# When eight weight pieces are converted: w_out in batches 1 to 3 instead of 0 to 2

## The chip, the core and the metric

The kernel runs on one core of a Trainium2 chip. The metric is device time in microseconds (us): the median of several executions. A profiled execution gives, beside its own time, a trace of every engine: PE (matrix multiply) with PEld (its weight load), DVE (vector), ACT (scalar), POOL (GpSimd) and SP (which here only issues DMAs).

## The reference, cut to what matters

Three stages follow each other. Attention works on 8 batches of 8 heads, 512 tokens and 32 state rows; it gives 4,608 rows of 512. A mixture of experts sends every row through one of 8 experts and scales it. A bilinear block ends it:

```python
xread  = softmax(scale * x @ state.T) @ state
sread  = softmax(scale * state @ x.T) @ x
x      = rows of concat([xread, sread])          # 4608 x 512
e      = argmax(x @ w_gate);  x = gate * (relu(x @ w1[e]) @ w2[e])
out    = (((x @ wa) * (x @ wb)) @ w3) @ w_out
```

`w3` is 1024 x 1024 and `w_out` 1024 x 512, and nothing non-linear stands between them, so the kernel multiplies them with each other first (`wo = w3 @ w_out`) and uses the product in the last block. Weights such as `w3` and `w_out` arrive as 64-bit floats and must be turned into 32-bit floats on the chip.

## The kernel before

**Stages.** Attention comes first, one pass of a loop over the batches `b` = 0 to 7. Routing of the rows follows, then the experts, then the bilinear block. PE multiplies in pairs of a high and a low part (`split` makes the pair from an f32 tile: a copy on ACT, a subtraction on DVE or POOL).

**The loop over batches.** Each pass emits seven steps in the order given by `order`, "xswrguf": `x` loads the tokens of batch b+3 (4 DMAs, buffer of 4 batches, so x of batch 4 needs batch 0's buffer back, which `read(0)` gives back); `s` is `softmaxes(b+1)` (transposes, scores, exponentials; DVE takes the maxima and sums); `w` loads and converts rows of `w3` (list `w3`: one eighth in batches 1, 2, 3, two in 4, one in each of 5, 6, 7, each as two halves of 128x512); `r` is `read(b)` (transposes of the weights of attention, products, `x_rows` written); `g` the gates of the state rows; `u` loads and converts pieces of `w_out`, those that list `wu` gives to this batch; `f` fuses an eighth of `w3` with all of `w_out` (one in batch 5, two in batch 7, five more during routing).

**A piece.** `load_w_out(i)` issues one DMA of 512 KB on SP into a `raw` buffer (`wu_raw`, 3 buffers shared with the halves of `w3`), and `convert` makes f32 of it: on ACT `Abs` into `wu_top` (L225) and a scaled copy into the f32 tile (L239), on DVE a maximum (L228), a shift (L230) and a merge (L233), on POOL an integer addition (L240). `split_w_out` then copies it on ACT (L177) and subtracts (L178) on DVE for pieces 0 and 5, on POOL for the six others. The f32 tiles (`wst`) have two buffers. Halves of `w3` go through the same `convert` as `w_raw` and `w_top`. The first reader of the finished pieces is the product `pwo` of the first `fuse`.

**What sets the order.** The program is not run in the order in which it is emitted. The tile framework plans it: every instruction has a place in emission order, shifted by `prio` (softmaxes and reads 300 places ahead, `w` 300 places back, `u` unshifted); a planner walks through the whole program in planned time and gives each engine the best-placed instruction that it thinks ready. Each engine's list is then fixed, and the chip runs each list strictly in order: an instruction that waits holds back all that stand behind it on its engine.

```python
prio = kn("prio", [0] * 7)
for b in range(B):
    for c in kn("order", "xsurgwf"):
        p_ = prio["xsurgwf".index(c)]
        with tc.high_priority(offset=p_) if p_ else ExitStack():
            steps[c](b)
```

Of the kernel before, what the change touches and what calls it, by code (L numbers as in the profile page):

```python
# [52 lines left out]
def tile_attention_moe_bilinear(  # L53
# [21 lines left out]
    B, H, S, D = x.shape  # L75
# [8 lines left out]
    NTT = NT // P  # L84
    NX = B * NC_
    SCALE = 1.0 / float(D) ** 0.5
    KN = {'e_wu': ['vector', 'gpsimd', 'gpsimd', 'gpsimd', 'gpsimd', 'vector', 'gpsimd', 'gpsimd'], 'prio': [0, 300, 0, 300, 0, -300, 0], 'w3b': 11, 'q_sr': 'sync', 'e_an': ['gpsimd', 'gpsimd'], 't_psr': 'B', 't_pl': 'B', 'q_wo': 'sync', 'wu': [0, 0, 0, 1, 1, 1, 2, 2], 'early': 7, 'ohb': 17, 'q_raw': 'sync', 'e_sT': ['vector', 'scalar'], 'e_tr': ['scalar', 'any', 'any', 'vector'], 'b_top': 2, 'w3': [1, 2, 3, 4, 4, 5, 6, 7], 't_psl': 'C', 't_pw3': 'A', 't_pst': 'C', 'b_sT': 2, 't_pS': 'A', 'b_a2': 1, 'e_add': ['gpsimd', 'gpsimd', 'gpsimd', 'gpsimd', 'gpsimd', 'gpsimd'], 'b_aT': 6, 'q_xr': 'sync', 'b_xr': 4, 'b_h': 10, 'q_std': 'sync', 'q_an': 'gpsimd', 'e_low': ['vector', 'gpsimd'], 't_pxr': 'CB', 'e_abs': 'scalar', 'ahead': 1, 'b_a': 1, 't_psT': 'A', 'b_xT': 1, 'fuse': [5, 7, 7, 7], 'e_xT': ['any', 'any', 'vector', 'any'], 'order': 'xswrguf', 'ahead0': 2}
    def kn(name, default):
        return KN.get(name, default)

# [219 lines left out]
    with ExitStack() as c1:  # L310
# [122 lines left out]
        wu = [fu.tile([P, KF, DM], F32R, name=f"wu{i}", bufs=1) for i in range(2)]  # L433
# [257 lines left out]
        prio = kn("prio", [0] * 7)  # L691
# [882 lines left out]
```

## Time and profile before

| | us |
|---|---|
| median of 3 runs (1165.36 to 1170.16) | 1168.14 |
| the profiled execution | 1171.04 |
| its span, first to last instruction | 1169.1 |
| PE busy in it | 1118.7 |
| DVE, ACT, POOL busy in it | 664.0, 450.7, 398.2 |

How to read it: the span is the part of the profiled execution that the trace covers; all starts in the trace are counted from its beginning. Attention fills about the first 145 us, routing the time to about 190 us, experts and bilinear block the rest. A busy share over the whole span mixes these stages, so the rows below are taken from stretches.

### The profile page before, as it was taken

How to read it: one execution, taken by the hardware profiler on the slowest of the kernel's cores; microseconds unless marked ns; L12 is line 12 of the kernel's file. 1: busy time of each engine (PE TensorE's matmuls, PEld its weight loads, DVE VectorE, ACT ScalarE, POOL GpSimd, SP SyncE). 2: the span in 40 equal slices, each digit the busy share in tenths (PEclk: the TensorE clock that was granted, in tenths of full speed). 3: DMA queues.
4: the chain of work that ended last, by engine and by line, in shares of the span. 5: the costliest groups of instructions: out<-in, count | busy, mean ns of one | idle time of the engine just before them, and what ended most of it. 6: DMA issues, size and time to landing. Idle time of an engine off the chain costs nothing. (4 is left out here: it accounts for less than half of the span.)

```text
span 1169.1 us, 18224 instructions
## 1 busy us (share of the span) xinstructions
PE 1118.7 (96%) x6880; PEld 982.7 (84%) x6880; DVE 664.0 (57%) x1206; ACT 450.7 (39%) x807; POOL 398.2 (34%) x383
## 2 busy tenths in 40 slices
PE   6888998999999999999999999999999999999995
PEld 4666777999999999987888888898888889889994
DVE  4999787636464546464855547343644545463341
ACT  3778644435454545454413223121412322131121
POOL 2555326114140322132001434623543453344222
PEclk9899999999999999999999999999999999999998
DMA  7786425546566666677414645443544445343431
GB/s 227 223 254 200 160 96 209 201 153 228 187 228 211 215 216 201 233 221 242 158 35 176 248 152 199 171 174 141 205 174 160 156 180 189 135 181 132 184 127 57
DMA packets 85008, 211.55 MB, mean 181 GB/s; under 512 B 12976, under 2 KB 42672, under 8 KB 79920
## 3 DMA queue, kind: packets, MB, share of 16 engines
q1 hardware_dynamic: 62256, 167.53, 42.2%
q10 hardware_dynamic: 17024, 24.42, 5.7%
q0 software_dynamic: 5632, 18.35, 4.5%
q8 instruction: 56, 0.92, 0.3%
q14 instruction: 40, 0.33, 0.1%
HBM read 166.23 MB, written 44.04 MB: 180 GB/s over the span
## 5 line engine op out<-in xcount | busy, mean ns | idle before, releaser
L183 PE MATMUL p<-w_x,w 128*128 128x448 f32 (+1 forms) x1638 | 338.6, 360 | 0.0
L183 PEld LDWEIGHTS p<-w_x,w 128*128 128x128 f32 x1638 | 303.7, 188 | 25.4
L183 PE MATMUL py<-h,w 128*128 128x288 f32 (+1 forms) x1152 | 197.9, 329 | 3.0 <-ACT y L1087 3.0
L183 PE MATMUL ph<-x,w 128*128 128x288 f32 (+2 forms) x1248 | 196.5, 316 | 2.9 <-DVE h L1025 2.7
L183 PEld LDWEIGHTS ph<-x,w 128*128 128x128 f32 x1248 | 179.4, 188 | 15.6 <-DVE h L1025 4.4
L183 PEld LDWEIGHTS py<-h,w 128*128 128x128 f32 x1152 | 173.8, 188 | 19.2 <-ACT y L1087 4.6
L178 DVE TENSOR_TENSOR w<-raw,w 128x1024 fp32r<-128x1024 f32 x80 | 96.9, 1237 | 74.6 <-ACT w L177 72.5
L1434 POOL TENSOR_TENSOR ab<-u,s 128x448 f32<-128x448 f32 (+1 forms) x40 | 47.6, 1189 | 259.3 <-DVE u L1432 170.4
L183 PE MATMUL po<-w_wo,aa 128*128 128x512 f32 x480 | 125.3, 393 | 1.9 <-ACT aa L177 1.0
L183 PEld LDWEIGHTS po<-w_wo,aa 128*128 128x128 f32 x480 | 89.7, 188 | 18.8 <-DVE aa L178 1.7
L177 ACT CAST w<-raw 128x1024 fp32r<-128x1024 f32 x80 | 81.6, 1050 | 51.6 <-DMA raw<-in_moe_w 46.8
L177 ACT CAST ab<-ab 128x384 fp32r<-128x384 f32 (+1 forms) x40 | 19.7, 493 | 184.4 <-POOL ab L1440 174.0
L240 POOL TENSOR_TENSOR wab<-wab,wab_top 128x512 int32<-128x512 int32 x16 | 20.7, 1292 | 179.5 <-DVE wab_top L233 151.5
L183 PE MATMUL po<-w_wo,ab 128*128 128x512 f32 x336 | 79.6, 391 | 0.4 <-DVE o L1466 0.4
L183 PEld LDWEIGHTS po<-w_wo,ab 128*128 128x128 f32 x336 | 62.9, 188 | 13.9 <-DVE o L1466 0.8
L997 POOL DMA_INDIRECT xg<-x_rows,gidx x38 | 45.7, 1202 | 83.3 <-PE pxg L1003 66.7
L1437 DVE TENSOR_TENSOR u<-u,p 128x448 f32<-128x448 f32 (+1 forms) x40 | 24.3, 606 | 84.4 <-PE p L183 84.3
L1438 POOL TENSOR_TENSOR ab<-u,s 128x448 f32<-128x448 f32 (+1 forms) x40 | 48.3, 1208 | 49.2 <-DVE u L1437 49.2
L1025 DVE SCALAR_TENSOR_TENSOR h<-ph,h 128x288 fp32r<-128x288 f32 (+2 forms) x104 | 51.2, 502 | 20.8 <-ACT h L1024 20.3
L1024 ACT ACTIVATE h<-ph 128x288 fp32r<-128x288 f32 (+2 forms) x104 | 44.5, 447 | 42.6 <-PE ph L183 30.8
L183 PE MATMUL pwo<-wu,w3T 128*128 128x512 f32 x192 | 50.2, 411 | 3.4 <-POOL w3T L178 2.9
L1440 POOL TENSOR_TENSOR ab<-ab 128x448 f32<-128x448 f32 (+1 forms) x40 | 48.9, 1222 | 3.1
(291 smaller groups left out, 1441.0 us busy)
## 6 DMA issues: line engine op xcount, KB each, us to landing
w<-w_rows SPq DMA_DIRECT2D x39, 1792.0 KB
raw<-in_moe_w SPq DMA_DIRECT2D x80, 512.0 KB
x<-in_x SPq DMA_DIRECT2D x32, 256.0 KB
w_raw<-in_moe_w SPq DMA_DIRECT2D x16, 512.0 KB
x_rows<-xr SPq DMA_DIRECT2D x32, 256.0 KB
w_rows<-wh_s ACTq DMA_DIRECT2D x32, 256.0 KB
y<-y_T SPq DMA_DIRECT2D x8, 896.0 KB
w_rows<-wh_w ACTq DMA_DIRECT2D x32, 192.0 KB
```

What stands on the lines that cost most here:

```text
L177: nc.scalar.copy(hi, src)
L178: (engine or nc.vector).tensor_tensor(lo, src, hi.bitcast(F32), op=ALU.subtract)
L183: m = nc.tensor.matmul(o, l[a], r[b], start=start and i == 0, stop=stop and i == 2)
L240: nc.gpsimd.tensor_tensor(wi, wi, top, op=ALU.add)
L997: gathered = nc.gpsimd.indirect_dma_start(out=x[0:r], out_offset=None, in_=x_rows, in_offset=bass.IndirectOffsetOnAxis(ap=gidx[0:r, t - s0 ...
L1024: nc.scalar.activation(hl[0], src, AF.Relu)
L1025: nc.vector.scalar_tensor_tensor(out=hl[1], in0=src, scalar=0.0, in1=hl[0].bitcast(F32), op0=ALU.max, op1=ALU.subtract)
L1434: gpsimd(b2, u3, s5, op=ALU.add)
L1437: vector(u4, u2, p3, op=ALU.add)
L1438: gpsimd(a2, u4, s5, op=ALU.add)
L1440: gpsimd(ab[:, n : 2 * n], a2, b2, op=ALU.mult)
```

## The change

One list of settings changes: the eight pieces of `w_out`, given to batches 0, 0, 0, 1, 1, 1, 2, 2 before, are given to 1, 1, 1, 2, 2, 2, 3, 3. No instruction is added or removed, no engine, queue or buffer changes.

```diff
-    'wu': [0, 0, 0, 1, 1, 1, 2, 2]
+    'wu': [1, 1, 1, 2, 2, 2, 3, 3]
```

The list is used where batches are given their pieces and where the loop emits them:

```python
for i, b_ in enumerate(kn("wu", [0, 0, 1, 1, 2, 2, 3, 3])):
    WU[b_].append(i)
...
"u": lambda b: ([(load_w_out(i), split_w_out()) for i in WU[b]]),
```

## Rows read from the trace of the kernel before

**Rows 1.** The page: busy time of each engine, share of the span, instructions.
```profile
PE 1118.7 (96%) x6880; PEld 982.7 (84%) x6880; DVE 664.0 (57%) x1206; ACT 450.7 (39%) x807; POOL 398.2 (34%) x383
```

**Rows 2.** Windows: stretch, length, busy PE, PEld, DVE, ACT, POOL, granted clock, DMA share, GB/s.
```profile
23.00:42.00 19.00, 13.40 (x146) 10.17 (x144) 13.90 (x32) 13.10 (x27) 7.46 (x6) 0.73 0.57 190
42.00:117.00 75.00, 63.74 (x745) 46.11 (x745) 74.97 (x203) 60.42 (x130) 40.91 (x36) 1.00 0.75 231
```

**Rows 3.** Timeline of ACT: start, length, line, operation, idle before it and releaser.
```profile
26.21 0.66 ACT L225 ACTIVATE wu_top<-wu_raw 128x512 f32<-128x512 f32 x1 [5.83 <-DMA wu_raw<-in_moe_w_out]
...
28.58 1.06 ACT L140 COPY a2T<-pa2T 128x512 f32<-128x512 f32 x2
```

**Rows 4.** Timeline of DVE around pieces 0 to 2, and of later scores.
```profile
21.55 0.41 DVE L556 TENSOR_SCALAR_CACHE_REDUCE sT<-psT 128x256 f32<-128x256 f32 x1
...
26.90 0.43 DVE L228 TENSOR_SCALAR wu_top<-wu_top 128x512 f32<-128x512 f32 x1 [3.90 <-ACT wu_top L225]
...
36.69 0.67 DVE L178 TENSOR_TENSOR wu<-wu,wu 128x512 fp32r<-128x512 f32 x1
...
42.78 0.41 DVE L556 TENSOR_SCALAR_CACHE_REDUCE sT<-psT 128x256 f32<-128x256 f32 x1
...
105.05 0.41 DVE L556 TENSOR_SCALAR_CACHE_REDUCE sT<-psT 128x256 f32<-128x256 f32 x1
```

**Rows 5.** Timeline of PE: the stall, the first fuse, the last read.
```profile
23.75 0.49 PE L576 MATMUL pS<-ident,sT 128*128 128x128 f32 x3
29.20 1.94 PE L632 MATMUL psr<-x,a2T 128*32 128x64 f32 x64 [4.96 <-ACT a2T L140]
...
121.73 5.15 PE L183 MATMUL pwo<-wu,w3T 128*128 128x512 f32 x21
...
138.20 1.10 PE L632 MATMUL psr<-x,a2T 128*32 128x64 f32 x64
```

**Rows 6.** Timeline of SP's queue: DMA issues.
```profile
19.14 1.41 SPq L208 DMA_DIRECT2D wu_raw<-in_moe_w_out  x3
31.20 1.92 SPq L328 DMA_DIRECT2D x<-in_x  x4
...
123.17 0.33 SPq L208 DMA_DIRECT2D w_raw<-in_moe_w  x1
```

**Rows 7.** Tile wu_top: durations in ns, least, median, most, first and last start.
```profile
L228 DVE TENSOR_SCALAR wu_top<-wu_top x8: 411/427/1530, 26.9 to 80.8; 128x512 f32<-128x512 f32 x8
L230 DVE TENSOR_SCALAR wu_top<-wu_top x8: 364/416/817, 29.2 to 82.6; 128x512 int32<-128x512 int32 x8
L233 DVE SCALAR_TENSOR_TENSOR wu_top<-wu_raw,wu_top x8: 677/684/1531, 31.0 to 84.8; 128x512 int32<-128x512 int32 x8
```

**Rows 8.** Windows of DVE on wu_top alone: busy, clock, DMA; last their sum.
```profile
23.00:42.00 19.00, 5.29 (x9) 0.73 0.57 190
...
sum 79.00, DVE 15.98; mean DVE 3.20
```

**Rows 9.** Windows on w_top alone: busy DVE, ACT, POOL, clock, DMA.
```profile
42.00:117.00 75.00, 21.46 (x33) 7.59 (x11) 14.60 (x11) 1.00 0.75 231
```

**Rows 10.** Timeline of POOL: the last subtraction of a piece.
```profile
90.53 1.44 POOL L178 TENSOR_TENSOR wu<-wu,wu 128x512 fp32r<-128x512 f32 x1
```

**Rows 11.** Windows of all engines around the stall, columns as in rows 2.
```profile
24.00:29.00 5.00, 0.24 (x3) 0.01 (x1) 1.36 (x4) 2.76 (x5) 0.00 (x0) 0.82 0.39 158
29.00:37.00 8.00, 7.15 (x83) 5.90 (x84) 8.00 (x17) 5.35 (x12) 5.48 (x4) 0.50 0.60 160
37.00:42.00 5.00, 5.00 (x52) 3.26 (x50) 4.54 (x12) 4.99 (x12) 1.98 (x2) 0.95 0.60 233
```

**Rows 12.** Waits of ACT from 42 to 130: total us, times, longest.
```profile
ACT w L239 <- DMA w_raw<-in_moe_w: 5.7, 6, 1.8
...
ACT wu L239 <- DMA wu_raw<-in_moe_w_out: 2.2, 2, 1.2
```

**Rows 13.** Waits of PE from 200 to the end, columns as in rows 12.
```profile
PE py L183 <- ACT y L1087: 3.0, 6, 0.9
PE ph L183 <- DVE h L1025: 2.7, 4, 0.9
```

More of the change, by code (lines that the diff above doesn't have):

```diff
@@ L86, in tile_attention_moe_bilinear @@
     SCALE = 1.0 / float(D) ** 0.5
-    KN = {'e_wu': ['vector', 'gpsimd', 'gpsimd', 'gpsimd', 'gpsimd', 'vector', 'gpsimd', 'gpsimd'], 'prio': [0, 300, 0, 300, 0, -300, 0], 'w3b': 11, 'q_sr': 'sync', 'e_an': ['gpsimd', 'gpsimd'], 't_psr': 'B', 't_pl': 'B', 'q_wo': 'sync', 'wu': [0, 0, 0, 1, 1, 1, 2, 2], 'early': 7, 'ohb': 17, 'q_raw': 'sync', 'e_sT': ['vector', 'scalar'], 'e_tr': ['scalar', 'any', 'any', 'vector'], 'b_top': 2, 'w3': [1, 2, 3, 4, 4, 5, 6, 7], 't_psl': 'C', 't_pw3': 'A', 't_pst': 'C', 'b_sT': 2, 't_pS': 'A', 'b_a2': 1, 'e_add': ['gpsimd', 'gpsimd', 'gpsimd', 'gpsimd', 'gpsimd', 'gpsimd'], 'b_aT': 6, 'q_xr': 'sync', 'b_xr': 4, 'b_h': 10, 'q_std': 'sync', 'q_an': 'gpsimd', 'e_low': ['vector', 'gpsimd'], 't_pxr': 'CB', 'e_abs': 'scalar', 'ahead': 1, 'b_a': 1, 't_psT': 'A', 'b_xT': 1, 'fuse': [5, 7, 7, 7], 'e_xT': ['any', 'any', 'vector', 'any'], 'order': 'xswrguf', 'ahead0': 2}
+    KN = {'e_wu': ['vector', 'gpsimd', 'gpsimd', 'gpsimd', 'gpsimd', 'vector', 'gpsimd', 'gpsimd'], 'prio': [0, 300, 0, 300, 0, -300, 0], 'w3b': 11, 'q_sr': 'sync', 'e_an': ['gpsimd', 'gpsimd'], 't_psr': 'B', 't_pl': 'B', 'q_wo': 'sync', 'wu': [1, 1, 1, 2, 2, 2, 3, 3], 'early': 7, 'ohb': 17, 'q_raw': 'sync', 'e_sT': ['vector', 'scalar'], 'e_tr': ['scalar', 'any', 'any', 'vector'], 'b_top': 2, 'w3': [1, 2, 3, 4, 4, 5, 6, 7], 't_psl': 'C', 't_pw3': 'A', 't_pst': 'C', 'b_sT': 2, 't_pS': 'A', 'b_a2': 1, 'e_add': ['gpsimd', 'gpsimd', 'gpsimd', 'gpsimd', 'gpsimd', 'gpsimd'], 'b_aT': 6, 'q_xr': 'sync', 'b_xr': 4, 'b_h': 10, 'q_std': 'sync', 'q_an': 'gpsimd', 'e_low': ['vector', 'gpsimd'], 't_pxr': 'CB', 'e_abs': 'scalar', 'ahead': 1, 'b_a': 1, 't_psT': 'A', 'b_xT': 1, 'fuse': [5, 7, 7, 7], 'e_xT': ['any', 'any', 'vector', 'any'], 'order': 'xswrguf', 'ahead0': 2}
     def kn(name, default):
```

## The prediction

> **What bounds the kernel.** I read the page first, then the windows of the first 200 us, then the engines' timelines where a window showed idle time, and last the waits. Over the span PE is busy 96% [rows 1], which suggests that work on DVE cannot matter. The windows correct that. From 42 to 117 us, in attention, DVE is busy 74.97 of 75 us while PE has 11.3 us free [rows 2]: in this stretch DVE sets the pace, and every microsecond of DVE work there is a microsecond of time, as long as the engine never waits. The conversions of w_out and w3 run in this same stretch.
>
> Just ahead of it, from 23 to 42 us, DVE is idle for 19 - 13.90 = 5.10 us [rows 2]. The timelines show why. ACT reaches the first operation of piece 0 (L225) and stands 5.83 us until its DMA has landed; the copies a2T that read(0) needs stand behind it in ACT's list and run at 28.58 [rows 3]. PE had finished the transposes at about 24.2 and waits 4.96 us for a2T; DVE waits 3.90 us for the same piece [rows 4, 5]. So in the kernel before, the very pieces that the change moves cause the one real stall of attention. That is the argument for a gain, and the question is whether moving the pieces to batch 1 takes them away from there.
>
> **What the change does, part by part.** Nothing is added or removed: per piece one DMA issue on SP, three operations each on ACT (L225, L239, L177) and DVE (L228, L230, L233, plus L178 for pieces 0 and 5), one or two on POOL. Only the place in the planning order falls, by one batch.
>
> *Whether pieces 0 to 2 start later.* In emission order their three DMAs are moved behind the loads of x for batch 4, the writes of read(0) and of softmaxes(2) on SP, and their operations behind those of softmaxes(2) and read(1) on every engine. But emission order is not issue order. The last half of w3 belongs to batch 7 and is put back by another 300 places, yet its DMA is issued at 123.17, 15 us before the read of batch 7 at 138.20 [rows 5, 6]. Work whose buffer is free is issued far ahead of its batch when nothing better placed is ready. At 19.14 that is the position of pieces 0 to 2: all three raw buffers are empty, and the next load of x is not issued before 31.20, since it needs the buffer that read(0) gives back at 29.20 or later [rows 5, 6]. I see nothing better placed for SP to issue then, nor for ACT, which sat idle, and the halves of w3 are placed further back still. So I take it that the three DMAs keep their place at about 19, ACT keeps L225 ahead of a2T, and the stall stays: a change of 0 us. The other end of this unknown is that they really go behind the loads of x; that is the first rival.
>
> *Pieces 3 to 7.* They already wait for raw buffers and for the two f32 tiles, not for their place. After them come in both kernels the same halves of w3. Where a piece is now beaten by an operation of softmaxes or of a read, it runs some operations later; DVE executes the same sum. Cost 0, as long as they are finished in time: the last subtraction ends at 90.53 + 1.44 = 91.97 and the first fuse starts at 121.73 [rows 5, 10], so 29.8 us cover the delay. From score to score a batch takes (105.05 - 42.78) / 4 = 15.6 us [rows 4]; a whole batch of delay uses half of the cover. Without this cover the fuse would wait for whatever is missing, but it needs two batches for that.
>
> *Who runs beside whom.* The same 128x512 operation takes 0.41 us at best and 1.53 at worst (L228), and L230 and L233 spread in the same manner [rows 7]. Over the eight pieces DVE spends 15.98 us on wu_top [rows 8], and at the medians it would be 8 x (0.427 + 0.416 + 0.684) = 12.2: 3.8 us are lost to something beside them. A new order can remove these 3.8 or double them. I take 0, since neither engine's amount of work changes, and keep plus and minus 3.8 us as the bounds. The Trainium skill, page "SBUF — State Buffer", section "Who interferes with whom", says that DVE and GpSimd share one port pair under an exclusive lock, and that the later of the two stands still. By that rule the long operations are those that met POOL, and moving a piece moves the meeting with it; the trace gives no number that contradicts it.
>
> The sum for the likeliest case is 0 + 0 + 0. Against the profiled execution (1171.04, span 1169.1, with 1.9 us outside the span) nothing changes; that execution is 2.9 us above the median of the runs, 1168.14, which is the scale of the forecast: 1168 us, with 1164.3 to 1171.9 as this case's own range.
>
> **Rival A: the pieces do start a batch later and the stall goes.** SP's list would have the pieces behind the load of x that starts at 31.20, 12 us later than now. For it: a later place is what the change asks for. Against it: the early issue of the last half of w3. Price: from the scores at 21.55 to the next at 42.78 are 21.2 us [rows 4]. DVE's idle 5.10 us would go, but also the 5.29 us on wu_top and 0.67 us of piece 0's subtraction [rows 4, 8], 5.96 us in all, which must then be done in the stretch where DVE is full. That alone is -5.10 + 5.96 = +0.9 us. The granted clock adds to the gain: it is 0.82 in the stretch with the wait, 0.50 (1.2 GHz) from 29 to 37 and 0.95 after it, and PE is busy 7.15 us at the low level [rows 11]; without its idle 4.96 us before, this work would take half, 3.6 us less. The step of 21.2 us would shrink to 21.2 - 5.1 - 3.6 = 12.5 and the sum is -8.7 + 5.96 = -2.7: 1165.4 us. The page "TensorE: Matmul & The Clock Gate" of the Trainium skill, section "What's actually happening", says that the low clock is the default and activity releases it, so that the gap itself costs the clock. By that rule the value is -2.7, without it +0.9. The best end is a step that DVE's attention work alone fills: from 42 to 117 this is 74.97 - 21.46 for w_top - (15.98 - 5.29) for wu_top = 42.8 us [rows 2, 8, 9], in 75 / 15.6 = 4.8 steps, 8.9 us each. Then -12.3 + 5.96 = -6.4 us: 1161.8. It is faster by over 0.5% (5.84 us) only if the step falls below 9.4 us.
>
> **Rival B, the other side: the wait moves instead of going.** One of the moved pieces gets its place in ACT's list ahead of its own DMA, as piece 0 has now, but in a batch where DVE is full. Price: a wait of 5.83 us cost 5.10 us of DVE time [rows 2, 3]; one such more gives 1168.1 + 5.1 = 1173.2 us. For it: from 42 to 130 ACT already waits for DMAs of these conversions, 5.7 and 2.2 us in total [rows 12], with DMA busy 0.75 of the stretch [rows 2]. Against it: the longest of these waits is 1.8 us and DVE's other work covers them all. It makes the kernel slower by over 0.5% when a single wait reaches 5.84 + 0.73 = 6.6 us with the same cover.
>
> **Rival C: later stages shift.** A slightly different end of attention changes the lists behind it. From 200 us on PE waits 3.0 + 2.7 = 5.7 us for the two main evacuations of the experts [rows 13]; if they double or vanish, the time is 1173.8 or 1162.4. Nothing speaks for either sign.
>
> **Chances and range.** The likeliest case, order and stall unchanged, has 0.62, with 0.05 left at either end for more than 5.84 us (several of the small effects in one direction). Rival A has 0.16, of which 0.06 below -5.84; rival B 0.13, of which 0.06 above +5.84; rival C 0.09, split evenly, nearly all of it within what the others leave, and I count 0.04 beyond 0.5% on each side. So faster is 0.05 + 0.06 + 0.04 = 0.15, slower 0.05 + 0.06 + 0.04 = 0.15, within 0.5% 0.70; 0.5% is about what a measurement of this kernel can tell from no change. The range reaches from just under rival A's best end (1161.8) to just over rival B's and C's (1173.8): 1161 to 1174. No more than 2 in 10 is left outside.
>
> **What the profile would show.** If I am right, SP issues three wu_raw at about 19 us, ACT waits 5 to 6 us at L225, PE about 5 us at psr before 30 us, and the granted clock falls to 0.50 behind it; DVE stays full to about 117, and the first pwo starts within 2 us of 121.73. Rival A shows as a first wu_raw after about 30 us, no wait of PE above 2 us before 40, and the clock at 1.00 there. Rival B shows as an ACT wait for wu_raw above 5 us with DVE idle in the same stretch after 42 us. Rival C shows as an unchanged start of the experts with other waits of PE after 200. The prediction is wrong in its main step if the first wu_raw moves.

## The result, and the profile after

The change makes the kernel slower by a little: 1174.94 us (median of 7, 1171.0 to 1179.42) against 1168.63 (median of 7, 1165.36 to 1170.78), ratio 1.0057 with a 95% interval of 1.0037 to 1.0077. I had forecast no change, 1168 us, and 1174 as the upper end.

The two profiled spans don't show this: 1169.2 us after, 1169.1 before. The execution of after that was profiled is its shortest (1171.0), that of before (1171.04) lies 2.4 us above the median given here. So I compare stages, by four events that every trace holds: the last gates of attention (second `psl<-wg`), the counts of routing (`pc`), the product that places the rows (first `psl<-codes`) and the first output product of the experts (first `py`).

First the rows that answer to the prediction. SP's queue of after, then its ACT and PE at the stall:

```profile
18.81 0.94 SPq L208 DMA_DIRECT2D w_raw<-in_moe_w  x2
19.80 0.43 SPq L208 DMA_DIRECT2D wu_raw<-in_moe_w_out  x1
31.57 1.41 SPq L328 DMA_DIRECT2D x<-in_x  x3
...
34.34 0.89 SPq L208 DMA_DIRECT2D wu_raw<-in_moe_w_out  x2
```

```profile
25.91 0.66 ACT L225 ACTIVATE w_top<-w_raw 128x512 f32<-128x512 f32 x1 [6.04 <-DMA w_raw<-in_moe_w]
...
28.96 1.06 ACT L140 COPY a2T<-pa2T 128x512 f32<-128x512 f32 x2
```

```profile
29.58 1.93 PE L632 MATMUL psr<-x,a2T 128*32 128x64 f32 x64 [5.84 <-ACT a2T L140]
```

Against [rows 3, 5, 6] the stall is still there: ACT waits 6.04 us instead of 5.83, PE 5.84 instead of 4.96. But ACT waits for another transfer: two halves of w3, which belong to batch 1 in both kernels, now take raw buffers ahead of the pieces. Only the first piece keeps its place (19.80 against 19.14); pieces 1 and 2 come at 34.34, 15 us later and behind the load of x.

Windows of after, columns as in [rows 2]; then DVE's waits from 42 to 117 (total us, times, longest):

```profile
23.00:42.00 19.00, 11.85 (x141) 8.65 (x140) 13.73 (x32) 11.69 (x24) 6.88 (x6) 0.82 0.55 193
42.00:117.00 75.00, 66.84 (x740) 47.64 (x738) 72.64 (x202) 59.96 (x128) 41.95 (x36) 0.98 0.72 230
```

```profile
DVE sT L556 <- PE psT L548: 1.1, 2, 0.9
DVE xT L140 <- PE pxT L532: 0.5, 2, 0.3
DVE wu_top L228 <- ACT wu_top L225: 0.5, 1, 0.5
```

In [rows 2] DVE is busy 74.97 of the 75 us of attention; now 72.64. It is idle 2.36 us; the view lists 2.1 us of waits, 1.6 of them for PE, and for the kernel before the same view is empty. How a wait of PE turns into one of DVE is to be seen at one place. PE and DVE of after, windows around it, and last PE of before at the same transposes, which follow there without a gap:

```profile
80.61 0.49 PE L614 MATMUL psrT<-ident,sr 128*128 128x128 f32 x3
83.21 0.63 PE L532 MATMUL pxT<-ident,x 128*128 128x128 f32 x4 [2.11 <-issue]
```

```profile
81.02 1.49 DVE L228 TENSOR_SCALAR w_top<-w_top 128x512 f32<-128x512 f32 x1
82.43 0.68 DVE L581 TENSOR_TENSOR a<-pS,m 128x512 f32<-128x512 f32 x1
```

```profile
80.00:84.00 4.00, 1.89 (x29) 1.59 (x19) 4.00 (x8) 3.41 (x8) 1.65 (x1) 1.00 0.63 211
84.00:88.00 4.00, 4.00 (x16) 3.19 (x15) 3.68 (x8) 2.84 (x8) 1.33 (x1) 0.57 0.90 264
```

```profile
79.94 0.49 PE L614 MATMUL psrT<-ident,sr 128*128 128x128 f32 x3
80.27 1.04 PE L532 MATMUL pxT<-ident,x 128*128 128x128 f32 x8
```

PE's next transposes start when DVE has read scores out of PSUM (L581), and that read stands behind a conversion of w3 (L228, 1.49 us) in DVE's list. The profile calls the 2.11 us "issue"; that L581 is the releaser is my reading of the times, 82.43 + 0.68 = 83.11. Behind that idle time the granted clock is 0.57 for four microseconds (most of them at 1.2 GHz), PE is busy all of them, and DVE, which was full from 80 to 84, is idle 0.32 us there.

The larger part lies behind attention. PE from the gates to the codes product, first of after, then of a second trace of before:

```profile
146.56 1.06 PE L670 MATMUL psl<-wg,srT 128*128 128x16 f32 x8
147.48 11.45 PE L183 MATMUL pwo<-wu,w3T 128*128 128x512 f32 x48
158.76 0.18 PE L752 MATMUL pc<-cnt,ones 128*128 128x8 f16 x1
...
168.51 5.84 PE L183 MATMUL pwo<-wu,w3T 128*128 128x512 f32 x24
175.70 0.73 PE L183 MATMUL pwo<-wu,w3T 128*128 128x512 f32 x2 [1.34 <-ACT w3T L177]
177.21 3.06 PE L183 MATMUL pwo<-wu,w3T 128*128 128x512 f32 x12 [0.78 <-POOL w3T L178]
180.11 1.26 PE L276 MATMUL psl<-codes,ohlo 128*128 128x38 f16 x17
```

```profile
143.75 1.06 PE L670 MATMUL psl<-wg,srT 128*128 128x16 f32 x8
144.66 9.09 PE L183 MATMUL pwo<-wu,w3T 128*128 128x512 f32 x38
153.59 0.18 PE L752 MATMUL pc<-cnt,ones 128*128 128x8 f16 x1
...
169.99 3.04 PE L183 MATMUL pwo<-wu,w3T 128*128 128x512 f32 x12 [0.81 <-POOL w3T L178]
173.41 0.48 PE L276 MATMUL psl<-codes,ohlo 128*128 128x38 f16 x13 [0.37 <-DVE codes L271]
```

Two things differ. Ahead of `pc` stand 48 products of the fuse (`pwo`) instead of 38, 11.45 us instead of 9.09, and routing on DVE waits for `pc`: 3.33 us in after, 1.83 in the second trace of before (1.80 in the first).

```profile
159.01 0.17 DVE L758 TENSOR_SCALAR nq<-pc 128x8 int32<-128x8 f32 x1 [3.33 <-PE pc L753]
```

And the codes product of before is released by DVE (0.37 us of idle ahead of it), while in after it has nothing to wait for but the 12 pwo in front of it, which themselves waited for their operand.

The table has the events in us, the time that DVE is idle between 42 and 117 (75 less the busy time), and how many pwo stand between gates and `pc`. "Gates to codes" is the handover from attention to routing. "Clock" is the granted clock of PE, first from 42 us to the gates, then from gates to codes. "Traced" is the time of the execution that the trace shows; it can lie several us beside the median, and the columns behind it belong to that execution. The ratios are estimates from all runs of the two kernels; they aren't the quotients of the medians and lie up to 0.0012 (1.4 us) beside them.

| kernel | median | ratio to before (95%) | traced | DVE idle | gates | pwo | gates to codes | clock | first py |
|---|---|---|---|---|---|---|---|---|---|
| before | 1167.8 to 1168.8 |  | 1171.0 | 0.03 | 145.0 | 38 | 29.7 | 1.00, 1.00 | 225.2 |
| b_again | 1166.0, one run |  | 1166.0 | 0.19 | 143.8 | 38 | 29.7 | 1.00, 1.00 | 222.4 |
| after | 1174.9 | 1.0057 (1.0037 to 1.0077) | 1171.0 | 2.36 | 146.6 | 48 | 33.6 | 0.98, 1.00 | 230.2 |
| a_again | 1177.7 | 1.0067 (1.0043 to 1.0090) | 1179.2 | 2.58 | 148.2 | 48 | 37.5 | 0.97, 0.91 | 235.3 |
| p02 | 1175.3 | 1.0055 (1.0036 to 1.0073) | 1174.5 | 1.45 | 152.7 | 38 | 29.7 | 0.95, 1.00 | 233.0 |
| p37 | 1170.9 | 1.0018 (1.0004 to 1.0032) | 1165.9 | 0.35 | 144.1 | 38 | 29.6 | 1.00, 1.00 | 222.8 |
| u_first | 1176.9 | 1.0061 (1.0040 to 1.0082) | 1176.6 | 3.63 | 146.2 | 48 | 34.0 | 0.98, 1.00 | 231.7 |
| jog_uord | 1175.9 | 1.0071 (1.0048 to 1.0093) | 1178.7 | 4.02 | 148.8 | 48 | 33.8 | 0.97, 1.00 | 234.3 |
| jog_r | 1175.9 | 1.0072 (1.0051 to 1.0092) | 1175.7 | 3.22 | 147.0 | 48 | 35.4 | 0.97, 0.95 | 231.6 |
| jog_u | 1173.0 | 1.0041 (1.0029 to 1.0053) | 1172.4 | 2.01 | 150.4 | 38 | 29.7 | 0.98, 1.00 | 229.1 |
| jog_f | 1168.7 | 1.0004 (0.9989 to 1.0018) | 1169.4 | 0.06 | 145.0 | 38 | 29.6 | 1.00, 1.00 | 226.1 |
| h2_a | 1173.3 | 1.0044 (1.0027 to 1.0062) | 1177.7 | 1.65 | 149.7 | 36 | 30.1 | 0.97, 1.00 | 233.5 |
| f2_b | 1172.7 | 1.0039 (1.0022 to 1.0056) | 1175.1 | 0.19 | 144.0 | 24 | 32.3 | 1.00, 0.95 | 230.0 |
| f2_a | 1175.4 | 1.0062 (1.0039 to 1.0086) | 1176.0 | 4.34 | 150.0 | 24 | 32.6 | 0.97, 0.95 | 233.4 |
| nostall_b | 1175.8 | 1.0080 (1.0052 to 1.0107) | 1171.2 | 4.14 | 143.7 | 48 | 33.8 | 0.98, 1.00 | 227.2 |
| nostall_a | 1173.2 | 1.0038 (1.0023 to 1.0053) | 1175.4 | 2.52 | 144.1 | 48 | 35.0 | 0.97, 0.95 | 230.6 |
| nodve_b | 1168.1 | 1.0001 (0.9987 to 1.0015) | 1173.1 | 5.85 | 145.8 | 38 | 29.6 | 0.98, 1.00 | 226.0 |
| nodve_a | 1171.4 | 1.0034 (1.0018 to 1.0051) | 1171.9 | 6.30 | 142.0 | 48 | 35.3 | 0.98, 0.95 | 226.3 |

From the first py to the end of the execution every kernel takes 940.8 to 947.1 us, in no order that goes with its median; the second trace of before has 943.6, that of after 943.9. The loss is made ahead of the first py. The mean of two traces each: attention ends 3.0 us later, the handover takes 35.5 instead of 29.7 us, 5.9 more (the difference of the unrounded means), and from the codes to the first py it is 49.8 us in both. That makes 8.9 us of the stages against 6.3 and 9.1 us between the medians. Behind the first py after's two executions are 2.3 us shorter in the mean than before's, which leaves the 6.6 us between the four executions.

The clock column sorts the kernels. In the traces with a clock of 1.00 from 42 us to the gates (before twice, p37, jog_f, f2_b) attention ends at 143.8 to 145.0. In the traces of after (both), p02, u_first, jog_uord, jog_r and jog_u the clock there is 0.95 to 0.98, and attention ends at 146.2 to 152.7. (The kernels without the stall or without the pieces' DVE work have less to do there; they have 0.97 to 0.98 and 142.0 to 145.8.) The handover is 29.6 to 29.7 us wherever 38 pwo stand ahead of `pc`; with 48 it is 33.6 to 34.0 us at a clock of 1.00, 35.0 to 35.4 at 0.95 and 37.5 at 0.91. The form with 48 has 110 pwo in the handover as a whole, the other 98, so twelve stand there that else come behind the codes, ten of them ahead of `pc`. By this the price has three parts: PE's waits in attention with the low clock behind them, the twelve pwo, and the low clock that may follow their late operands. This is an ordering of 18 traces; no run holds the clock fixed.

### The profile page after: what moved, and what is told of

The parts are those of the page before. It is cut to its first block, busy times and chain, and to the rows that moved or that the text cites. A ratio compares the mean times of both kernels' runs of the same rounds, so it can differ in the third digit from the quotient of the medians.

```text
span 1169.2 us, 18229 instructions
## 1 busy us (share of the span) xinstructions
PE 1120.0 (96%) x6880; PEld 983.6 (84%) x6880; DVE 664.4 (57%) x1207; ACT 449.6 (38%) x806; POOL 396.6 (34%) x383
## 5 line engine op out<-in xcount | busy, mean ns | idle before, releaser
L183 PEld LDWEIGHTS p<-w_x,w 128*128 128x128 f32 x1638 | 303.7, 188 | 25.3
L997 POOL DMA_INDIRECT xg<-x_rows,gidx x38 | 42.5, 1120 | 87.2 <-PE pxg L1003 79.5
```

The source lines that it names most:

```text
L183: m = nc.tensor.matmul(o, l[a], r[b], start=start and i == 0, stop=stop and i == 2)
L997: gathered = nc.gpsimd.indirect_dma_start(out=x[0:r], out_offset=None, in_=x_rows, in_offset=bass.IndirectOffsetOnAxis(ap=gidx[0:r, t - s0 ...
```

## The experiments

**The changed kernel again, and the change in two halves.** A second trace of after, then pieces 0 to 2 alone and pieces 3 to 7 alone:

```diff
 'wu': [1, 1, 1, 2, 2, 2, 3, 3]   # after
+'wu': [1, 1, 1, 1, 1, 1, 2, 2]   # p02: only pieces 0 to 2 moved
+'wu': [0, 0, 0, 2, 2, 2, 3, 3]   # p37: only pieces 3 to 7 moved
```

> The changed kernel once more, for its time and for a second trace of it. If the loss is the change's own, the ratio to the kernel before is 1.004 to 1.008, and the trace places the some 6 us: theory 1 (attention: halves of w3 now take the raw buffers ahead of the pieces, and other waits come with that order) has the start of the routing counts (pc, 154.83 before) 3 to 7 us later; theory 2 (the stages behind attention: their lists differ and PE waits more there) has pc within 1 us of before and the experts or the bilinear block longer. If the seven runs were chance, the ratio is 0.998 to 1.002.

> Only pieces 0 to 2 are moved (batches 1,1,1,1,1,1,2,2). The first half of w3 is then converted ahead of piece 0, as in the changed kernel, and later pieces keep their batch. If the early swap costs the time, the ratio is 1.004 to 1.008; if the pieces of batches 2 and 3 cost it, 0.998 to 1.002.

> Only pieces 3 to 7 are moved (batches 0,0,0,2,2,2,3,3). Everything up to about 40 us is as before, then the halves of w3 of batch 2 go ahead of pieces 3 to 5. If the later pieces cost the time, the ratio is 1.004 to 1.008 with a wait of PE near 80 us; if the early swap costs it, 0.998 to 1.002.

The loss repeats. The two halves don't add up: pieces 3 to 7 alone cost 2.3 us, pieces 0 to 2 alone 6.7, and by another way than the whole, with the handover of before (29.7) and an attention that ends 7.7 us later. So there is no price per piece. The traced execution of p37 is its shortest, 5.0 us below its median, and shows nothing of its loss. In p02 more than half of the delay of attention is a stretch in which PE is busy at little over half the clock; by this row it loses about 10.16 x (1 - 0.54) = 4.7 us there, an estimate:

```profile
91.00:102.00 11.00, 10.16 (x70) 7.42 (x70) 10.66 (x29) 4.86 (x11) 7.54 (x7) 0.54 0.74 214
```

How one list can give two times is to be seen where read(1) needs its a2T. ACT, PE and the windows from 48 to 52, of the first trace of after, then of the second:

```profile
45.61 0.67 ACT L239 ACTIVATE w<-w_raw 128x512 int32<-128x512 uint32 x1 [1.99 <-DMA w_raw<-in_moe_w]
46.90 0.63 PE L614 MATMUL paT<-ident,an 128*128 128x128 f32 x4 [2.17 <-ACT a2T L140]
48.00:52.00 4.00, 4.00 (x71) 3.29 (x60) 4.00 (x7) 4.00 (x10) 2.55 (x2) 1.00 0.80 268
```

```profile
46.90 0.67 ACT L239 ACTIVATE w<-w_raw 128x512 int32<-128x512 uint32 x1 [2.61 <-DMA w_raw<-in_moe_w]
48.18 0.83 PE L614 MATMUL paT<-ident,an 128*128 128x128 f32 x4 [2.92 <-ACT a2T L140]
48.00:52.00 4.00, 3.82 (x74) 3.35 (x75) 4.00 (x9) 4.00 (x10) 1.69 (x2) 0.57 0.52 184
```

ACT waits for a half of w3, a2T stands behind it, PE waits for a2T: the stall of [rows 3, 5] in small, at a later batch. Where ACT's wait is 0.6 us longer, four microseconds at a mean clock of 0.57 follow. The second trace of after also shows the handover at its worst, PE, its clock, and DVE behind it:

```profile
170.16 5.84 PE L183 MATMUL pwo<-wu,w3T 128*128 128x512 f32 x24
178.51 1.22 PE L183 MATMUL pwo<-wu,w3T 128*128 128x512 f32 x2 [2.50 <-ACT w3T L177]
181.03 4.84 PE L183 MATMUL pwo<-wu,w3T 128*128 128x512 f32 x12 [1.30 <-POOL w3T L178]
185.72 0.60 PE L276 MATMUL psl<-codes,ohlo 128*128 128x38 f16 x17
```

```profile
178.00:181.00 3.00, 1.22 (x2) 0.50 (x2) 3.00 (x6) 1.92 (x3) 2.41 (x2) 0.53 0.03 13
181.00:186.00 5.00, 4.97 (x23) 3.81 (x24) 1.65 (x5) 2.28 (x4) 1.22 (x1) 0.60 0.15 56
```

```profile
185.94 1.46 DVE L275 TENSOR_SCALAR ohlo<-lane,lo 128x128 f16<-128x128 f16 x2 [3.35 <-PE psl L276]
```

PE runs out of pwo whose operand is there, waits 2.50 and 1.30 us, and the granted clock falls to 0.53 and 0.60 behind the gap. The same 12 pwo that took 3.06 us in the first trace take 4.84, and DVE, which has the codes ready, stands 3.35 us for PE. The same list gives 21.4 or 25.3 us from `pc` to the codes; before's gives 19.8 in both of its traces.

**Who takes the raw buffers first.** After, with the steps of a batch emitted in an order that has the pieces ahead of the halves of w3; beside it the same order with the pieces in batches 0 to 2:

```diff
-'order': 'xswrguf'
+'order': 'xsuwrgf'   # u_first: with after's wu; jog_uord: with before's wu
```

> All pieces in batches 1 to 3 as in the changed kernel, but each batch emits its pieces ahead of its part of w3 (order x,s,u,w,r,g,f), so that SP's list begins with pieces 0 to 2 again, as in the kernel before. Theory 1 (who takes the buffers first costs the time): 0.998 to 1.002. If the later batch alone costs it, 1.004 to 1.008.

> The kernel before with its pieces in batches 0 to 2, but with the steps of one batch put on the list in the order in which the run with the pieces ahead of the halves of w3 had them. With the three kernels at hand it makes a two by two table of batch and of order. Theory 'place of the pieces': as before, 1166 to 1170 us, and the later batches cost 6 to 8 us in either order. Theory 'order of the list': slower than before by 2 us or more, 1170 us and up, and the batches of the pieces cost less here than in the first order.

In u_first SP issues the three pieces first again, and nothing is won: the theory that the buffers explain the loss falls. The two kernels make the table complete. In the first order the later batches cost 6.3 and 9.1 us (6.7 and 7.8 by the ratios); in the second 1176.9 stands against 1175.9, with intervals of the ratios that overlap almost entirely. What batch the pieces belong to has no measurable price there; the other order alone, with the pieces where they were, costs as much as the change.

**Shifts of the list that don't touch the pieces' batches.** The ranks that stand for emission places are moved by ten, one step at a time:

```diff
-'prio': [0, 300, 0, 300, 0, -300, 0]
+'prio': [0, 300, 0, 310, 0, -300, 0]    # jog_r
+'prio': [0, 300, 10, 300, 0, -300, 0]   # jog_u
+'prio': [0, 300, 0, 300, 0, -300, 10]   # jog_f
```

> The kernel before with its w_out pieces where they are (batches 0 to 2) and one constant of the planner's order moved by a hair: the rank of the r steps from 300 to 310. It leaves all work in and shifts some hundreds of instructions against each other on TensorE, DVE and ScalarE. Theory 'order of the list' (the change lost its 6 us not by where the pieces stand but because any other list leaves DVE idle for some us more ahead of the routing): this is slower too, by 3 to 9 us: 1171 to 1177 us, with the first py at 228 to 234 us instead of 225. Rival 'place of the pieces': nothing of theirs has moved, 1166 to 1170 us.

> The kernel before with the rank of the u steps, those that load and convert the pieces of w_out, from 0 to 10, their batches as they were. 266 rows of TensorE's list, 480 of DVE's, 306 of ScalarE's differ. Theory 'order of the list, by DVE': slower than before by 3 to 9 us, with 48 pwo between the gates and pc and ten behind the first ph as in the other slower kernels, and the codes product later than 177 us. If it keeps the form of the kernel before (38 and none): 1167 to 1171 us, as the kernel with pieces 3 to 7 alone moved.

> The kernel before with the smallest shift of the list that was found: the rank of the f steps from 0 to 10. DVE's and GpSimd's lists are the same, 26 rows of TensorE's list, 8 of ScalarE's and 9 of SyncE's (one store of w_out rows now behind the reads of the counts) differ. Theory 'order of the list, by DVE' (a list costs by the DVE idle that it leaves ahead of the routing): DVE's order has not changed, 1166 to 1170 us. Rival 'any shift at all costs 7 us': 1173 us and up.

jog_r reproduces the change: 7.1 us slower, DVE idle 3.22, 48 pwo ahead of `pc`, handover 35.4. jog_u shows one part alone: the handover is before's to a tenth, attention ends 5.4 us later, and the loss is 4.5 us. It was expected with 48 pwo if slower, or at 1167 to 1171 us if it kept 38; it kept 38 and takes 1173.0, so attention can lose alone. jog_f, whose DVE list is row for row that of before, has no measurable cost, which refutes "any shift at all costs 7 us". The stretch of attention in jog_f, jog_r and jog_uord, in this order:

```profile
42.00:117.00 75.00, 63.86 (x747) 46.14 (x745) 74.94 (x203) 60.46 (x131) 40.92 (x36) 1.00 0.75 232
```

```profile
42.00:117.00 75.00, 66.10 (x745) 47.94 (x740) 71.78 (x201) 58.85 (x129) 42.76 (x36) 0.95 0.75 237
```

```profile
42.00:117.00 75.00, 65.64 (x731) 46.10 (x730) 70.98 (x191) 58.02 (x126) 40.23 (x35) 0.95 0.72 224
```

DVE has work for 75 us and does 71 to 72 of it; PE is busy longer for no more products, since the clock is 0.95 in the mean.

**The kernel before, a second trace.**

> The kernel before, unchanged, profiled a second time: how far its stages move from one execution to the next. If the stages up to the first py are a property of the list, pc comes at 153 to 156 us, the codes product at 174 to 176 us and the first py at 223 to 227 us again, and the rest takes 940 to 946 us. If they are as loose as the whole time is from run to run (1164 to 1173 us), a difference of 5 us in the first py between two kernels says little.

The events lie 1.2 us earlier than in the first trace up to the codes and 2.8 at the first py, a little more than expected there. The intervals between them repeat: 9.84 and 19.82 us from gates to `pc` to codes, in both.

**The products ahead of the counts.** The third group of w_out products is put behind the counts, whole (f2) or its second half (h2):

```diff
-    'fuse': [5, 7, 7, 7]
+    'fuse': [5, 7], 'fused': 2     # f2_b with before's wu, f2_a with after's
...
-                fuse(f, nc.gpsimd)
+                fuse(f, None if f == 2 else nc.gpsimd)
```

```diff
-            "f": lambda b: [fuse(f) for f in FUSE[b]],
+            "f": lambda b: [fuse(f, None, 0 if f == 2 else None) for f in FUSE[b]],   # h2_a
...
+        with tc.issue_after(counted.ins):
+            fuse(2, None, 1)           # the second half, 12 pwo
```

> The kernel before with one edit: the third group of w_out products (fuse(2)) is issued behind the routing counts instead of from batch 7 on. In the kernel before 38 pwo matmuls stand ahead of pc on TensorE, some of them of fuse(2). Theory 'TensorE's list' (the change cost what it cost because ten more pwo, 2.35 us, stand ahead of pc and the last ten come after the first ph): taking pwo from ahead of pc moves pc earlier by up to 2 us, and gives them back later, where TensorE waits for the routing anyway: 1164 to 1169 us. Rival 'attention step' (the loss is DVE's order in batches 3 to 5, which this edit leaves as it is): pc where it was, 1168 us. Rival 'jog' (any shift of the plan costs 3 to 9 us): 1172 to 1177 us.

> The changed kernel with the same edit: fuse(2) behind the routing counts. Theory 'TensorE's list': the 48 pwo ahead of pc become 32 or so, pc comes 3 to 4 us earlier than in the changed kernel (158.8 and 160.4 us there), and most of the loss of 6 us is gone: 1169 to 1171 us. Rival 'attention step': pc comes earlier by less than 1 us since its operand, not its place, is late: 1174 to 1177 us. Rival 'jog': no bound, but not nearer to before than to the changed kernel.

> The changed kernel with the second half of the third group of w_out products (12 pwo, their four transposes and the split of w3T) put behind the counts, so that pc has at most 36 to 38 pwo between the gates and itself, as in the kernel before. If the ten pwo ahead of pc (2.35 us) are part of the price as such, the time falls to 1171 to 1173 us. If DVE's idle time ahead of the codes is what counts, and pc's place only decides where DVE idles, it stays at 1173 to 1178 us.

The theory that the pwo ahead of `pc` are the price as such falls with f2_b: 24 of them instead of 38, `pc` 4.3 us earlier than in the first trace of before, the codes product 1.7 us later, and 1172.7 us instead of the 1164 to 1169 expected. f2_a agrees: `pc` comes 2.3 and 4.0 us earlier than in the two traces of after, and the time stays at 1175.4. PE of f2_b:

```profile
150.52 0.18 PE L752 MATMUL pc<-cnt,ones 128*128 128x8 f16 x1
...
168.03 0.74 PE L183 MATMUL pwo<-wu,w3T 128*128 128x512 f32 x2 [1.72 <-ACT w3T L177]
169.54 6.94 PE L183 MATMUL pwo<-wu,w3T 128*128 128x512 f32 x22 [0.77 <-POOL w3T L178]
176.32 0.59 PE L276 MATMUL psl<-codes,ohlo 128*128 128x38 f16 x17
```

The pwo taken from in front of `pc` stand in front of the codes product: 22 in one piece, 6.94 us, after a wait of 1.72 us and at a granted clock of 0.72 from 170 to 176. h2_a spreads them, has 98 in the handover again, and takes 30.1 us for it, as before within half a microsecond; PE of h2_a, where the codes product waits for DVE again:

```profile
176.40 3.05 PE L183 MATMUL pwo<-wu,w3T 128*128 128x512 f32 x12 [0.88 <-POOL w3T L178]
179.81 0.48 PE L276 MATMUL psl<-codes,ohlo 128*128 128x38 f16 x13 [0.36 <-DVE codes L271]
```

But what h2_a gains there it loses at once. From the codes to the first py it takes 53.7 us, where after and before take 49.0 to 50.6, so that from the gates to the first py it has 83.8 us, as the first trace of after (83.7). f2_b has the same 53.7. The kernel as a whole takes 1173.3 us, at the border between the two outcomes expected; its ratio, 1.0044, overlaps with both of after, so a gain isn't shown. Its traced execution is 4.4 us above its median, and the attention that ends at 149.7 in it needn't be typical.

**Without the stall at 24 to 29 us.** The first three conversions' ACT operations go behind read(0)'s copies a2T, both on ACT:

```diff
-                a2T = transposed(f"a2T{b}_{g}", ..., g)
+                a2T = transposed(f"a2T{b}_{g}", ..., g if b else 0)
+                if b == 0 and g == 1:
+                    held.append(copied[-1])
...
+        with tc.issue_after(held[0].ins) if held and turns[0] < 3 else ExitStack():
+            return convert(w, raw, pool, name, temps)
```

> The kernel before with the stall at 24 to 29 us taken away: the ScalarE copies that open the first three conversions of w_out are issued behind the second a2T copy of batch 0, and both a2T copies of batch 0 are ScalarE's. If the stall was on the path, the 5 us of TensorE's wait for a2T and the 5.1 us of DVE idle at 23 to 42 us go: sT of the third step starts near 38 us instead of 42.8, and the time is 1163 to 1166 us. If it was covered, because TensorE then falls to a clock of 0.50 as it did behind the stall, or because DVE's work is only put off: 1167 to 1170 us.

> The changed kernel with the stall at 24 to 29 us taken away in the same way. Its stall is there as in the kernel before (TensorE waits 5.8 us for a2T). If what the change costs is bound up with the stall and what is queued behind it, the two kernels without the stall agree within 2 us. If the loss is made later, in batches 3 to 7 and at the handover to the routing ('attention step', 'TensorE's list'), this one stays 5 to 8 us behind nostall_b.

The stall goes: `psr` starts at 23.67 instead of 29.20 [rows 5], the third step's scores at 35.49 instead of 42.78 [rows 4]. By the last gates 1.3 us of these 7.3 are left, or none against the second trace of before (143.72 and 143.75): DVE is idle 4.14 us in the stretch where it was full, and PE is full from there to the gates in before as well (second trace of before, 27.86 of 28 us):

```profile
117.00:145.00 28.00, 27.86 (x286) 21.49 (x279) 21.44 (x64) 18.11 (x42) 10.28 (x9) 1.00 0.46 155
```

The handover has 48 pwo and 33.8 us, and the time is 7.9 us above before, worse than either expectation; the traced execution is the shortest, 4.5 us below the median, and shows only part of it. nostall_a is faster than nostall_b by 2.6 us: they neither agree within 2 us nor lies nostall_a behind, as "made later" expected. That fits a price of the list and not of the pieces.

**Without the pieces' DVE work.** The three DVE operations of each piece are left out, so that the values of w_out are not the reference's:

```diff
+        if not name.startswith("wu_"):
             nc.vector.tensor_scalar(top.bitcast(F32), ..., op0=ALU.max)         # L228
             nc.vector.tensor_scalar(top, top, 3, 0x3FFFFFF8, ...)               # L230
             nc.vector.scalar_tensor_tensor(out=top, in0=high, ...)              # L233
```

> The kernel before without three DVE operations (L228, L230, L233) in each of the eight pieces of w_out, 24 operations of 0.43 to 0.69 us, about 12 us of DVE: the values of w_out are therefore not the reference's. If DVE's list up to the routing sets the time, the first py comes 8 to 12 us earlier, 1156 to 1162 us. If TensorE's own work sets it, the gain is less than 4 us.

> The changed kernel without the same 24 DVE operations, whose output is likewise not the reference's. Theory 'the pieces' DVE work collides with attention in the later batches': with that work gone, the two kernels agree within 2 us. Theory 'order of the list': the difference has no reason to vanish, and may have any size between 0 and 9 us; if the path is DVE's, both gain about the same 8 to 12 us.

In the trace of nodve_b, its longest execution (5.0 us above the median), DVE has 10.0 us less to do up to the codes (137.2 against 147.2), and all of it turns into idle time (38.3 against 27.5); the codes come at 175.5 instead of 174.7. Neither kernel gains the 8 to 12 us that were expected of a DVE path. The change costs 3.3 us between these two, again with the two forms of handover, 29.6 and 35.3; so a loss is left without these operations of the pieces. One reservation: leaving work out gives a new list too. Compared row by row (operation and tiles, the 24 left out), 77 rows of PE and 79 of DVE stand elsewhere in nodve_b than in before, about as many as in p02 (55 and 80). What is shown is that the two together gain nothing, not that the work alone is free.

## Why the prediction was wrong, step by step

*Whether pieces 0 to 2 start later.* The stall stays, as forecast, but by luck: the reason given was wrong. ACT waits 6.04 us, PE 5.84 for a2T, and the granted clock falls behind it, to 0.75 in 29 to 37 (0.50 in [rows 11]). But "the three DMAs keep their place at about 19" holds for one of them, two moved by 15 us, and "the halves of w3 are placed further back still" is false: two halves go first, and the wait is for them. The sign that was named for a wrong step, a first wu_raw that moves, couldn't show this, since the first one stayed. In batch 1 the halves are emitted ahead of the pieces, and their 300 places did not put them behind. u_first shows that this mistake was not the price.

*Pieces 3 to 7.* The last subtraction ends at 98.56 + 1.46 = 100.02 and the first fuse starts at 122.19, so the cover holds with 22.2 us. The cost is 2.3 us in place of 0 (p37, by its interval 0.5 to 3.7).

*Who runs beside whom.* This term stayed within its 3.8 us. From 23 to 117 DVE spends 15.40 us on wu_top against 15.98 [rows 8], and on w_top 3.77 + 19.62 = 23.39 against 0.63 + 21.46 = 22.09 [rows 9]; DVE's sum up to the codes is 148.5 (150.3 in the second trace) against 147.2. The reading of the long operations fits the trace of before: all five of wu_top on DVE above 0.8 us (L228 at 55.18 and 60.13, L230 at 62.23, L233 at 31.59 and 58.71) begin while an operation of POOL is running.

```profile
sum 94.00, DVE 15.40 ACT 5.60 POOL 10.82; mean DVE 7.70 ACT 2.80 POOL 5.41
```

*The step that failed* is the sum "0 + 0 + 0". It prices the change by DVE's work alone, from the premise "every microsecond of DVE work there is a microsecond of time, as long as the engine never waits", and so puts at nothing two things that an order decides. The first is the condition of its own premise: the engine does wait, DVE is idle 2.36 and 2.58 us where it was full, the clock falls behind some of PE's gaps (2.11 us in after, 2.92 in a_again), and attention ends 3.0 us later. The second is a stretch that the sum doesn't contain, from the gates to the codes: twelve pwo more stand there (110 instead of 98), ten of them ahead of `pc`, and it takes 5.9 us more. (3.0 and 5.9 are differences between the means of two traces each.)

The work itself is nearly unchanged. "No engine changes", in the section on the change, isn't quite true: the planner also chooses the engine of some copies, and one copy of aT has moved from ACT to DVE (1207 and 806 instructions against 1206 and 807 [rows 1]). In p02, p37, u_first, jog_uord, jog_r and jog_u two to six copies of 0.4 to 0.7 us have changed engines, in jog_f none. Compared row by row (line, operation and tiles), 160 rows of PE and 124 of DVE stand elsewhere in after than in before.

In [rows 2] DVE's 74.97 of 75 us looked like a bound. That 10 us less of DVE work bring nothing in nodve_b speaks against it, with the reservation made there; PE, with 63.74 of the same 75 us and full from 117 on, isn't far behind. The Trainium skill, page "Perfetto Trace Analysis", section "Identifying the Most-Contended Engine", takes the occupancy of the vector engine as the way to find the bottleneck and as a fair measure of how near it is to its roofline. Read for this stretch, that points to DVE, and nodve_b's time doesn't bear it out.

*The rivals.* Rival A came about by half: pieces 1 and 2 stand behind the load of x, and the stall stays. Rival B had the right sign and part of the mechanism: a wait of ACT for a transfer with a2T behind it did move to 45 us, but it is one for a half of w3, 1.99 and 2.61 us instead of 5.83, DVE stays busy over it (6.00 of 6 us from 42 to 48 in after), and its price is a gap of PE and, in one of two traces, the clock. Rival C's "different lists" were the right idea in the wrong place: from the codes on nothing is lost, while the handover, between attention and the experts, was in none of my cases.

The slow stretches shown here follow a gap of PE: 0.50 in [rows 11], 0.57 behind 2.11 us in after, 0.57 behind 2.92 us and 0.53 and 0.60 behind 2.50 and 1.30 us in a_again. The 12 pwo of a_again take 4.84 - 3.06 = 1.8 us longer for it, so a wait of PE can cost more than its own length. The Trainium skill, page "TensorE: Matmul & The Clock Gate", section "What's actually happening", has the low clock as the default that activity releases; these rows agree.

*What stays open.* Which single exchange in the lists costs the time in attention wasn't isolated: every edit that moves one row of DVE moves many, and jog_f, the only one that moves none, shows no more than that this list is enough. Whether the pieces in batches 1 to 3 could have a list as good as before's wasn't tried; the overlap of u_first and jog_uord speaks for it. Why the planner puts 38 pwo ahead of `pc` in one list and 48 in another stays open too. No kernel with all the work beats the one before.

## What to carry to other kernels

When a planner writes the lists, a change of place is a change of the whole list, and its price is that of a new list and not of the moved work: here six of the seven lists that differ from before's in DVE's order by a change of place alone cost 4.5 to 9.1 us (the seventh 2.3), and the one that left DVE's order cost 0.3. Such a neutral shift is the measure to hold an edit against. Before pricing work on an engine that looks full, ask whether the kernel would gain if the work were gone; a 99.96% share can be a good fit between two engines and no bound. And look at the handover between stages: count what stands in the matmul list in front of each product on the routing chain, since bulk products whose operands come late hold it back by their length and, in some executions, by the clock behind their wait. Moving them behind one product puts them ahead of the next, as f2_b and h2_a showed.

## What the hardware showed that I had not expected

The same 12 products of 128x512 took 3.04 to 3.06 us at full granted clock and 4.84 at 0.60, in the same program from one execution to the next: a_again's gap of 2.50 us was followed by a low stretch, after's of 1.34 us was not. The length of one gap doesn't decide it: 2.11 us at 81 us in after was followed by 0.57, 2.17 us at 45 us in the same trace and 2.04 us at 59 us in the second trace of before left the clock at 1.00, and in jog_uord it fell to 0.57 from 96 to 100 with no gap above 0.7 us in the ten microseconds before. And one list can hold its stages to a few hundredths (19.82 us from `pc` to codes in both traces of before), where another moves by 4 us (21.35 and 25.31), with nothing changed but the execution.
